# Mixed V written to DRAM and gathered back through the load queue, with the loads and the mixing weights rearranged around it

## The chip, the cores and the metric

The kernel runs on one core of one Trainium2 chip. The metric is the device time of one execution in microseconds (us), smaller being better. A profiled execution gives, beside it, a span (first to last recorded work) and a record of what each engine did. The engines are PE (TensorE matmuls), PEld (its weight loads), DVE (VectorE), ACT (ScalarE), POOL (GpSimd) and SP (SyncE). Loads from DRAM that convert fp32 to fp16 are issued from POOL; plain copies and transposing copies are issued from SP.

## The reference

Two stages follow each other. The first is a block-sorting attention over 4 batches, 8 heads, 768 positions and head size 64; the second a Fourier mixing layer with a layer norm and a two-layer perceptron.

```python
for _ in range(5):                      # P: [4, 8, 8, 8], softmax by rows, then by columns
    P = exp(P - max(P, -1)); P = P / sum(P, -1); P = P / sum(P, -2)
k_sorted = einsum('bhij,bhjcd->bhicd', P, k_blocks)   # blocks of 96 positions
v_sorted = einsum('bhij,bhjcd->bhicd', P, v_blocks)
attn = softmax(0.125 * q_block @ k_sorted_block.T)    # inside each block
x = (attn @ v_sorted_block)                           # -> [4, 768, 512]
mixed = real(fft(fft(x, axis=1), axis=2))
u  = x + mixed
un = (u - mean(u)) / sqrt(var(u) + 1e-6)
out = u + relu(un @ w_ch1) @ w_ch2                    # 512 -> 2048 -> 512
```

## The kernel before, in words

Nothing is written in the order in which it runs. Every step is added to a list (`P.add`) with the engines that may run it, what it reads and writes, a priority and an assumed duration. `Plan.schedule` then lays all steps out in time once, at build time, and the result is one fixed order of instructions per engine. On the chip each engine goes through its own order and waits wherever an input or a buffer isn't ready; later instructions of that engine wait with it. Loads are steps of POOL, plain and transposing copies steps of SP, so POOL's and SP's queues are such fixed orders too. If an assumed duration is wrong, the order stays as it was planned.

The 128 sorted blocks of two batches (2 x 8 heads x 8 blocks) are one group `t` of V. Group 0 serves batches 0 and 1, group 1 batches 2 and 3. The fp16 copy of the raw V has a partition for each source block, and 96 x 64 values in it; group 0 lies in `hr[0]`, group 1 in the first four slots of `kq`, once batch 0's keys and queries have been used.

- `v_path` (L665 on) sums V over its 96 positions: PE adds up pieces of 512 columns with an identity matrix (L675, 12 matmuls a group), DVE reduces the rest (L683) and makes the mean (`vb`, `vbn`). Then V is rearranged into `vcx`: group 0 by eight strided copies (helper line L660) on DVE and ACT, group 1 by eight DVE subtractions of the mean (L708).
- `bdv_make` (L743 on) turns the 8 x 8 sorting weights into block-diagonal matrices with PE (fp32 matmuls, L745) and DVE (L749), and copies them to fp16 (`bdv16`).
- `v_mix` (L713 on) mixes the blocks. For each head-dimension value d a matmul (L724) has the rearranged V as its weights, so that the output has the 96 positions on the partitions, which is what attention needs; group 0 has a second matmul for the mean (L727). Sixteen copies a group (L660, `vsf<-bank`) bring the result to `vsf`, where each block has 64 values and a constant column, a row of 65.
- `kqt` (L897) sorts and transposes the keys, `scores` (L952) multiplies, ACT takes the exponential (L961), DVE or ACT subtract one (L974, L976) and write `eb`, of which there are four. `av` (L991) multiplies with `vsf`, DVE divides (L1003, L1006) and writes `rt`.
- `a_path` and `a_rows` prepare low-rank terms of the transform, `dft1` (L1063 to L1073, with sums on DVE from L1023) and `dft2` (L1138 to L1153) do the two transforms; DVE adds `u` (L1160, L1172), makes statistics (L1186), POOL the inverse deviation (L1193 to L1202, list `lns`), and `un` is normalised (L1213, L1217) and transposed (L1232 by PE for batch 0, a transposing copy on SP for the others).
- `mlp` (L1253 first layer, L1274 second) runs per batch and half of its rows, at a low priority on PE: it fills PE where nothing more urgent is ready.

The loads of keys, queries, V, tables and the perceptron's weights all leave from POOL (L472) in the order keys, queries, V of group 0, further keys and queries, tables, batch 1, weights. Group 1 of V is loaded at about 36 to 40 us, the keys and queries of batches 2 and 3 after the second layer norm of batch 0.

Of the kernel before, what the change touches and what calls it, by code (L numbers as in the profile page):

```python
# [9 lines left out]
F32 = mybir.dt.float32  # L10
# [33 lines left out]
GT = 384  # L44


def _consts():
# [56 lines left out]
    vrow = np.zeros((1, 128, D + 1), f16)  # L104
# [9 lines left out]
    def as32(m):  # L114
# [8 lines left out]
                rows=rows, erow=np.tile(erow, (1, 4)), vrow=vrow, pack=pack)  # L123


class Op:
    __slots__ = ("n", "costs", "fn", "preds", "succs", "left", "ready", "prio",
                 "vts", "fresh", "nbytes", "end", "start", "eng", "tag",
                 "crit", "late")
# [13 lines left out]
class Plan:  # L143
# [14 lines left out]
    def add(self, costs, fn, r=(), w=(), prio=None, nbytes=0, tag="",  # L158
            after=()):
# [7 lines left out]
        o.preds, o.succs, o.vts, o.fresh = set(after), [], [], []  # L167
        for k in r:
            o.preds.update(self.wr.get(k, ()))
# [41 lines left out]
    def schedule(self):  # L211
# [48 lines left out]
        while todo:  # L260
# [70 lines left out]
            for s in o.succs:  # L331
                s.left -= 1
                for x in s.costs:
                    s.ready[x] = max(s.ready[x],
                                     o.end + (0.03 if x == e else self.XL))
# [30 lines left out]
def kernel(  # L366
# [22 lines left out]
    def many(name, n, shape, dtype):  # L389
# [18 lines left out]
    vcx = ct("vcx", [128, 128 * D + 2], F16)  # L408
    dtab = vcx[:, 6144:7168].rearrange("p (c w) -> p c w", c=4)
    lt = vcx[0:97, 7168:7168 + LTW]  # L410
    vsf = ct("vsf", [97, 128 * (D + 1)], F16)
    vsb = vsf[:, 0:128 * (D + 1)].rearrange("p (g w) -> p g w", w=D + 1)
    eb4 = ct("eb4", [97, 4, EW], F16)
    P.pool("eb", [eb4[:, n, :] for n in range(4)])
# [24 lines left out]
             vcx[:, 7938:8194].bitcast(F32).rearrange(  # L439
# [15 lines left out]
    pk = hr[1].rearrange("p a b -> p (a b)")[0:32, 0:1024].rearrange(  # L455
        "p (i x) -> p i x", i=NB)
    pv = hr[1].rearrange("p a b -> p (a b)")[0:32, 1024:3072].bitcast(
        F32).rearrange("p (i x) -> p i x", i=NB)
    pws = hr[1].rearrange("p a b -> p (a b)")[0:32, 3072:3232].bitcast(F32)
# [9 lines left out]
    def load(dst, src, nbytes, w, prio, eng="POOL", r=(), after=()):  # L469
# [3 lines left out]
                  prio=prio, nbytes=nbytes, tag="load", after=after)  # L473
# [3 lines left out]

    slot = {}
# [34 lines left out]
    def load_v(t, hf, prio):  # L513
        load(nat[t].rearrange("p (c d) -> p c d", d=D)[
            :, 48 * hf:48 * hf + 48, :],
            vv[128 * t:128 * t + 128, 48 * hf:48 * hf + 48, :], 1572864,
            [("nat", t, hf)] + (hk(0)[8 * hf:8 * hf + 8] if t == 0 else
                                kqk(2 * hf) + kqk(2 * hf + 1)), prio)
# [10 lines left out]
    for n in range(4):  # L529
        P.add({"POOL": (1.5, 1.6)}, lambda _, n=n: nc.gpsimd.memset(  # L530
            eb4[0:96, n, :], 0.0), w=[("ebz", n)], prio=-190.0, tag="ebz")
# [850 lines left out]
```

The softmax here doesn't subtract the row's maximum and nothing guards it: scores larger than these inputs give would overflow.

## Time and profile before

| what | us |
|---|---|
| median of 14 runs (lowest, highest) | 292.82 (290.82, 294.43) |
| the profiled execution, its own time | 293.97 |
| its span | 292.2 |
| PE busy, of the span | 261.9 |
| DVE busy | 171.3 |
| ACT busy | 157.8 |
| POOL busy | 67.7 |
| first-layer matmuls (L1253), 512 of them | 91.5 |
| second-layer matmuls (L1274), 384 of them | 87.9 |
| mixing of V on PE (L724 and L727), 192 of them | 21.2 |
| mixed V to `vsf` (DVE and ACT, 16 each) | 23.0 |
| subtraction of the mean, group 1 (L708), 8 of them | 11.8 |

A line of a group of instructions gives the line of the code, the engine, the operation, output and inputs, the shape, the count, then the busy time of all and the mean duration in ns of one, and last the idle time of the engine just ahead of them with what ended it. A line of a timeline gives start and duration of one or several equal instructions. Durations of neighbours on one engine overlap a little, so that the distance of two starts is what an instruction costs in a full stretch. A line of the table of stages gives the stage, then the busy time of each engine in it, the granted PE clock (1.00 is full), the mean busy share of the DMA engines and GB/s.

### The profile page before, as it was taken

What the parts mean: (1) busy time and instruction counts of PE and PEld (TensorE: products, weight loads), DVE (VectorE), ACT (ScalarE), POOL (GpSimd) and SP (SyncE); (2) the same over time, 40 slices, a digit from 0 to 9 for tenths busy, and PEclk for the clock granted to TensorE, in tenths of its full rate; (3) what the DMA queues carried; (4) which work ended last, traced back from release to release, by engine and by line L of the source; (5) the groups of instructions that cost most, each with busy time, mean ns of one, the idle gap of its engine ahead of it and who ended that gap; (6) DMA issues with size and microseconds to landing.
All of it is one profiled execution on the core that took longest, in us unless ns stands there. A gap on an engine that the chain in (4) does not pass through costs nothing.

```text
span 292.2 us, 5807 instructions
## 1 busy us (share of the span) xinstructions
PE 261.9 (90%) x2284; PEld 155.6 (53%) x2284; DVE 171.3 (59%) x405; ACT 157.8 (54%) x323; POOL 67.7 (23%) x104
## 2 busy tenths in 40 slices
PE   0289987797999999999999999999999999999980
PEld 0147976554566565554566456455555545545530
DVE  4476899999999999841479742145124226210020
ACT  2485979986778946881368027226514605425300
POOL 8974300003920460020320002023000212200021
PEclk9995999999999999999999999999999999999995
DMA  7999999910991499310112011311321111221001
GB/s 112 211 252 246 213 208 209 221 23 16 96 181 23 73 170 145 78 37 20 72 49 56 2 72 37 57 72 49 46 81 37 38 54 72 38 90 36 2 36 72
DMA packets 42529, 26.33 MB, mean 90 GB/s; under 512 B 30106, under 2 KB 38824, under 8 KB 42500
## 3 DMA queue, kind: packets, MB, share of 16 engines
q0 software_dynamic: 23536, 18.31, 37.2%
q1 hardware_dynamic: 18966, 7.64, 11.7%
q8 instruction: 18, 0.29, 0.4%
q14 instruction: 9, 0.07, 0.1%
HBM read 28.96 MB, written 6.29 MB: 121 GB/s over the span
## 4 chain that ended last, share of the span: by engine, by line
PE 70%; DVE 17%; DMA 7%; issue 3%; POOL 2%; POOLq 0%; ACT 0%; DVEq 0%
PE bank L1274 27%; PE bank L1253 27%; DMA hr<-in_v_dram 5%; DVE rt L1006 2%; PE bank L897 2%; DMA out_dram<-u,rows 2%; PE bank L724 2%; PE bank L991 2%; PE bank L952 2%; PE bank L1149 2%; DVE vsf L660 2%; DVE st L1186 1%; PE bank L1063 1%; DVE eb L974 1%; PE bank L1153 1%
## 5 line engine op out<-in xcount | busy, mean ns | idle before, releaser
L1265 ACT ACTIVATE hr<-bank 128x384 f16<-128x384 f32 x115 | 56.2, 490 | 75.3 <-PE bank L1253 74.5
L1253 PE MATMUL bank<-ut,w1sb 128*128 128x384 f16 x512 | 91.5, 326 | 0.7 <-ACT ut L660 0.7
L1274 PE MATMUL bank<-w2sb,hr 128*128 128x512 f16 x384 | 87.9, 379 | 0.0
L1253 PEld LDWEIGHTS <-w1sb 128*128 128x128 f16 x512 | 48.6, 98 | 34.5 <-issue 1.1
L1274 PEld LDWEIGHTS <-hr 128*128 128x128 f16 x384 | 36.7, 98 | 41.8 <-issue 0.2
L1282 DVE TENSOR_TENSOR u<-bank,u 128x512 f32<-128x512 f32 x24 | 16.5, 689 | 60.2 <-PE bank L1274 59.8
L961 ACT ACTIVATE ex<-bank 96x384 f32<-96x384 f32 x64 | 27.9, 485 | 6.5 <-PE bank L952 6.4
L1295 POOL DMA_INDIRECT out_dram<-u,rows x12 | 12.1, 1011 | 77.0 <-DVE u L1282 56.8
L1193 POOL TENSOR_SCALAR mv<-mv 128x3 f32<-128x3 f32 x8 | 1.9, 239 | 110.6 <-DVE mv L1188 110.6
L976 ACT ACTIVATE eb<-ex,negone 96x384 f16<-96x384 f32 x35 | 20.8, 615 | 0.2
L1213 ACT ACTIVATE un<-u,nm,ny 128x512 f16<-128x512 f32 x15 | 12.2, 810 | 11.5 <-DMA ut<-un 8.2
L472 POOL DMA_DIRECT2D kq<-in_q_dram x20 | 17.4, 896 | 1.7 <-DMA kq<-in_q_dram 1.2
L991 PE MATMUL bank<-vsf,eb 97*128 97x65 f16 x416 | 16.5, 194 | 1.3 <-DVE rr L836 0.5
L1172 DVE SCALAR_TENSOR_TENSOR u<-rt,bank 128x510 f32<-128x510 f16 x12 | 8.1, 680 | 16.3 <-PE bank L1138 8.9
L1006 DVE TENSOR_TENSOR rt<-bank,rz 128x384 f16<-128x384 f32 x32 | 17.3, 550 | 0.3
L991 PEld LDWEIGHTS <-eb 97*128 97x128 f16 x416 | 15.4, 98 | 3.6 <-issue 1.3
L927 PE MATMUL bank<-pack,qr 128*128 128x128 f16 x48 | 5.3, 264 | 13.3 <-ACT qr L660 12.8
L1186 DVE BATCH_NORM_STATS2 st<-u 128x6 f32<-128x512 f32 x24 | 16.1, 686 | 0.3
L1160 DVE SCALAR_TENSOR_TENSOR u<-rt,bank 128x512 f32<-128x512 f16 x12 | 8.0, 684 | 13.9 <-PE bank L1153 13.5
L724 PE MATMUL bank<-bdv,vcx 128*128 128x128 f16 (+1 forms) x128 | 12.7, 226 | 0.0
L952 PE MATMUL bank<-qt,ks 64*128 64x96 f16 x256 | 11.5, 209 | 1.3 <-DVE rt L1006 0.4
L660 DVE CAST vsf<-bank 96x512 f16<-96x512 f32 x16 | 11.5, 776 | 1.3 <-PE bank L727 1.2
(130 smaller groups left out, 342.3 us busy)
## 6 DMA issues: line engine op xcount, KB each, us to landing
kq<-in_k_dram POOLq DMA_DIRECT2D x8, 384.0 KB, 7.2
w1sb<-in_moe_w_ch_dram POOLq DMA_DIRECT2D x4, 512.0 KB, 15.4
w2sb<-in_moe_w_ch_dram POOLq DMA_DIRECT2D x4, 512.0 KB, 18.8
out_dram<-u SPq DMA_DIRECT2D x8, 256.0 KB, 2.0
kq<-in_q_dram POOLq DMA_DIRECT2D x4, 384.0 KB, 11.3
hr<-in_v_dram POOLq DMA_DIRECT2D x2, 768.0 KB, 12.3
kq<-in_v_dram POOLq DMA_DIRECT2D x2, 768.0 KB, 20.7
kq<-in_q_dram POOLq DMA_DIRECT2D x16, 96.0 KB, 5.3
```

Of the source, the lines that this page charges most:

```text
L472: o = P.add({eng: c}, lambda _: e.dma_start(dst, src), r=r, w=w, prio=prio, nbytes=nbytes, tag="load", after=after)
L660: (nc.scalar.copy if e == "ACT" else V.tensor_copy)(dst, src)
L724: nc.tensor.matmul(o, vcx[:, 96 * d:96 * d + m], bd, start=True, stop=(t == 1))
L952: nc.tensor.matmul(pss[h2].ap[:, BLK * j:BLK * j + BLK], ks.ap[rows, 4 * g + j, :], qt.ap[rows, c0:c0 + BLK])
L961: nc.scalar.activation(ex.ap, pss[h2].ap[0:96, 0:384], AF.Exp, scale=SCALE),
L976: nc.scalar.activation(ed, src, AF.Identity, bias=negone[0:96])
L991: nc.tensor.matmul(po.ap[:, 65 * T:65 * T + 65], eb.ap[:, e0:e0 + 128], vsf[:, vi:vi + 65], start=(n == 0), stop=(n == len(WIN[T]) - 1), s ...
L1006: P.add({"DVE": (0.45, 0.56)}, lambda _: V.tensor_tensor(rt.ap[:, :, D * h:D * h + D], po3()[:, :, 0:D], rz.ap[:, :, None].broadcast_to([1 ...
L1186: P.add({"DVE": (0.6, 0.69)}, lambda _, u=u, st=st: V.bn_stats(st.ap, u.ap), r=[u], w=[st], tag="bn")
L1253: nc.tensor.matmul(ps.ap[:, 0:GT], w1sb[:, c, 128 * fc:128 * fc + 128], ut.ap[:, c, :], start=(c == 0), stop=(c == 3))
L1265: nc.scalar.activation(hr[g][:, fc, :], ps.ap[:, 0:GT], AF.Relu)
L1274: nc.tensor.matmul(ps.ap, hr[g][:, fc, 128 * tt:128 * tt + 128], w2sb[:, fc, :], start=(fc == 0), stop=(fc == 15))
```

## The change

1. Mixing on PE uses the weights the other way round: the block-diagonal matrix is the stationary operand and V streams, 512 columns at a time. A group has 12 pieces (group 0 two matmuls for each, the second for the mean), and the output has the blocks on the partitions. The rearranging copies into `vcx` are gone, and `vcx` is small.
2. The result is therefore transposed as far as attention is concerned. It is copied to SBUF (`vm`: `hr[1]` for group 0, in place for group 1), written to DRAM by six copies on SP for each group, and gathered back into `vsf` by six transfers on POOL, each of 32 x 64 rows of 64 fp16 values. `av` of a batch waits for the three transfers of its half. Rows of `vsf` are 80 wide.
3. Loads: V of group 0 goes first, then the queries and keys of batch 0 and half of batch 1. Tables, the other half of batch 1 and the weights stand in POOL's queue behind the first three gathers (`gate`, `behind`).
4. V of group 1 is loaded after the second layer norm of batch 0, by six transfers of 128 x 16 rows of 64 values; its sum over positions moves from PE to four DVE reductions, and the subtraction becomes two instructions in place.
5. The mixing weights become fp16 parts: high and low halves come from the fp32 weights, PE multiplies both in fp16, and `bdv16` and `bdv32` both come straight from PSUM.
6. `eb` has six buffers instead of four; the clearing of two is on DVE. The sorting weights' scratch space moves from `hr[1]` to `rv`, `fo`, `eo` and `rr`. Priorities of `dft2` and of batch 1's low-rank terms change, and two of `dft2`'s matmul groups are held behind the third.

```diff
-    load_qk("k", 0, 0, -5000.0)
-    load_qk("q", 0, 0, -4999.0)
-    load_v(0, 0, -4998.0)
-    load_v(0, 1, -4997.0)
+    load_v(0, 0, -5000.0)
+    load_v(0, 1, -4999.0)
+    load_qk("q", 0, 0, -4998.0)
+    load_qk("k", 0, 0, -4997.0)
     load_qk("k", 0, 1, -4996.0)
     load_qk("q", 0, 1, -4995.0)
...
+    load_qk("k", 1, 0, -4994.0)
+    load_qk("q", 1, 0, -4993.0)
...
+        if t:
+            for n in range(4):
+                P.add({"DVE": (1.65, 1.75)}, lambda _, n=n: V.tensor_reduce(
+                    vb[:, 0, 16 * n:16 * n + 16],
+                    n3.rearrange("p c d -> p d c")[:, 16 * n:16 * n + 16],
+                    axis=AX.X, op=ALU.add),
+                    r=[("nat", 1, r) for r in range(6)] + stage, w=["vb"],
+                    tag="vb1")
...
+        for hf in range(2):
+            def f(_, hf=hf):
+                m = nat[1][:, 3072 * hf:3072 * hf + 3072].rearrange(
+                    "p (c d) -> p c d", d=D)
+                V.tensor_tensor(m, m, vbn[:, None, :].broadcast_to(
+                    [128, 48, D]), op=ALU.subtract)
...
-        for n in range(16):
+        for n in range(12):
+            r, hf = divmod(n, 2)
             ps = Buf("pm", "pf")
...
+                nc.tensor.matmul(o, bd, n4[:, r, 8 * hf:8 * hf + 8],
+                                 start=True, stop=(t == 1))
+                if t == 0:
+                    nc.tensor.matmul(
+                        o, bd, vbn[:, None, :].broadcast_to([128, 8, D]),
+                        start=False, stop=True)
...
+        for hb in range(2):
+            w64 = slice(64 * hb, 64 * hb + 64)
+            for k_ in range(3):
+                cols = slice(2048 * k_, 2048 * k_ + 2048)
+                P.add({"SP": (0.4, 4.2)}, lambda _, w64=w64, cols=cols:
+                      nc.sync.dma_start(vdr[t][w64, cols], vm[w64, cols]),
...
+                o = P.add({"POOL": (1.3, 1.3)},
+                          lambda _, k_=k_, w64=w64, cols=cols:
+                          nc.gpsimd.dma_start(
+                              vsb[32 * k_:32 * k_ + 32, w64, 0:D],
+                              vdr[t][w64, cols].rearrange(
+                                  "g (c d) -> c g d", d=D)),
...
-              + [("vsb", n) for n in range(16)], w=[po, (rts[b], "a", h)],
+              + [("vsb", n, b % 2) for n in range(3)],
...
+    gate = gets[0, 0][-1:]
+    for n, nm in enumerate(("dtab", "lt", "tab", "cs")):
+        load_c(nm, 25.0 + n)
+    load_qk("k", 1, 1, 31.0)
+    load_qk("q", 1, 1, 31.5)
...
+    gate = lns[1:2]
     load_v(1, 0, 60.0)
     load_v(1, 1, 61.0)
+    gate = ()
```

## The prediction

> **What bounds the kernel now.** I read the table of stages first, to see where PE is full and where it isn't.
>
> ```profile
> core 0: us, PE busy (x) PEld busy (x) DVE busy (x) ACT busy (x) POOL busy (x), PEclk, DMA share, GB/s
> 45.00:50.00 5.00, 3.79 (x73) 2.96 (x74) 5.00 (x16) 5.00 (x12) 0.00 (x0) 1.00 1.24 207
> 60.00:65.00 5.00, 4.44 (x59) 3.03 (x58) 5.00 (x11) 4.18 (x11) 0.00 (x0) 1.00 0.01 3
> 120.00:140.00 20.00, 20.00 (x147) 10.41 (x146) 8.30 (x19) 11.35 (x26) 2.71 (x5) 1.00 0.16 32
> ```
>
> There are two regimes. Up to some 75 us DVE is full (5.00 of 5.00) and PE has holes; afterwards PE is full and DVE isn't. The PE timeline has the border, the chain of waits the end (start, us, what):
>
> ```profile
> 73.20 1.46 PE L1253 MATMUL bank<-ut,w1sb 128*128 128x384 f16 x8 [0.67 <-ACT ut L660]
> ```
>
> ```profile
> 274.98 4.33 PE bank L1274 x20
> ```
>
> The last matmul ends at about 279.4; 12.8 us of output follow, to 292.2. From 73.2 to 279.4 are 206.2 us. PE's instructions behind the border, counted in the built order and priced by distances of starts in full stretches (L1253 3.90/24 = 0.163 us, L1274 7.77/36 = 0.216, the small ones likewise), need 202.2 us. So the span is the time of the first L1253, plus 202.2, plus some 4 of holes, plus 12.8. What must be forecast is the border, the work behind it, and the holes. For the border I read DVE's timeline and the start of the chain, which comes first here:
>
> ```profile
> 3.54 13.84 DMA hr<-in_v_dram
> ```
>
> ```profile
> 39.21 0.18 DVE L1003 RECIPROCAL rz<-bank 128x6 f32<-128x6 f32 x1
> 62.72 1.87 DVE L1160 SCALAR_TENSOR_TENSOR u<-rt,bank 128x512 f32<-128x512 f16 x3
> 69.16 0.55 DVE L1217 TENSOR_SCALAR un<-u,ny,nm 128x512 f16<-128x512 f32 x1
> ```
>
> V lands at 17.4, attention's first division comes at 39.2, the first u at 62.7, the first un at 69.2, the first layer 4.0 later.
>
> **What the Trainium skill says.** "DMA: Bandwidth & Descriptors" (Anatomy of one DMA) says that DMA engines don't wait on semaphores: the issuing engine waits, and what is queued on it waits too. The trace has it: POOL sits 15.9 us ahead of a key load, waiting for L724. The same section gives a fixed 2.0 us for a POOL-issued DMA; here they take longer, 4.5 to 5.4 us from the start of the issue for query loads of 96 KB, and the trace decides. Its "Two DMAs through the same engine are not ordered" says that a DMA reading what another wrote must wait for its semaphore: store and gather can't overlap. "TensorE: Matmul & The Clock Gate" (Part 1) says that PE runs at half rate until it has been busy for some 3.4 us; before 29 us a 512-column matmul takes 0.416 (2.50/6), later 0.216.
>
> **The change part by part.**
>
> *Loads first.* Two V loads now have nothing ahead of them. Before, the first query load had landed at 10.05, half of V at 13.7, all at 17.4: 1.57 MB each 3.67 us. So V lands at 13.7, 3.7 earlier; query and key of batch 0 at 15.5 and 17.4, all eight loads at about 25. The sorting weights no longer wait behind query copies on ACT (a hole of 2.99 on DVE) and are done at about 11.6, before V. Hidden by V.
>
> *Mean and weights.* Six matmuls after V's landing (2.5), the reduction 0.7, small work: `vbn` at 18.3. The fp16 weight matmuls replace fp32 ones of 0.29 each and lie beside query transposes; likewise two more DVE memsets lie where DVE waits for the first load. Nil; uncovered, 1 to 2 us.
>
> *Mix.* From about 18.7, 24 matmuls at 0.416 until the clock rises, then 0.216: 5.2 to 10 us. I take a rise at about 23 and the last copy at 26.6 (12 copies of 0.58 on ACT or 0.68 on DVE, rows of 64x512 casts). Removed: 128 matmuls, eight rearrangements (8.5 us on two engines) and 16 copies of 0.78; added those 12.
>
> *Store and gather.* No such row exists. Store: 256 KB output copies on SP land after 2.0; bounds 1.8 and 3; last of the first half at 28.8. Gather: 2048 rows of 128 B. Query loads have 768 such rows and leave POOL each 0.83 us, landing no later within a burst (POOL's timeline, then the DMA issues: count, size, us to landing):
>
> ```profile
> 79.01 3.32 POOL L472 DMA_DIRECT2D kq<-in_q_dram  x4
> ```
>
> ```profile
> kq<-in_q_dram POOLq DMA_DIRECT2D x4, 96.0 KB, 5.3
> ```
>
> So DMA passes at least 925 rows a us: at most 2.2 us for a gather; from the slope of the issue (512 rows 0.745, 768 rows 0.83) at least 1.4. A further 4.4 until landing. The third lands at 28.8 + 1.4..2.2 + 4.4 = 34.6 to 35.4. Meanwhile scores go on, which six `eb` permit. DVE's work from the first mix copy to the first division is 15.5 (5 copies of V, 4 of keys, 3 of queries, 7 subtractions, low-rank steps and others): from 19.6, not before 35.1. With holes while PE is cold I take 36.5 for the division, against 39.2: the gather is just hidden.
>
> *From there to u.* Before 23.5, all DVE. Gone from this stretch, by starts: four divisions 1.8 and reciprocals 0.4, two `bdk` 2.2, two query copies 1.8, two key copies 1.0, three subtractions 0.8, low-rank steps 1.0: 9.0, leaving 14.7. They don't vanish: part moved ahead, under the gather's latency, part behind the border, where DVE isn't full. With 0.5 for chain latency, u at 51.7. From u to un 6.4 and from un to the first L1253 4.0 as before: **62.1, not 73.2; 11.1 earlier.**
>
> *Loads behind the gathers.* Everything queued on POOL behind the third gather (tables, half of batch 1, second gathers, weights) starts at 30.6, not at 13.6. 3.1 MB at 0.43 MB/us, 4 to land: tables by 38, while the transform starts at about 46. Gathers, then 4.2 MB: first-layer weights by 56 to 58, second-layer by 66, wanted at 62 and 77. Hidden, with 4 us to spare at the tightest.
>
> *PE behind the border.* 64 mix matmuls of 0.056 (3.6) become 12 of 0.216 (2.6); 26 attention and 8 score matmuls, 1.0 together, slip behind the border. Again 202.2: nil.
>
> *Group 1.* Its loads now wait for the layer norm, border + 1. Six of 2048 rows: 8.4 to 13.2 on POOL, landing at +14 to +18.6; batch 2's keys and queries queue behind. Then four reductions of 1.5 to 1.9 (1536 values, from a copy of 768 at 0.75 and a reduction of 512 at 0.65), two residual sums queued between, 1.3: done at +22 to +27.5. The subtraction is 1.9 (four times a 768-value sum of 0.47) or 3.4 (a broadcast of 1024 at 1.12, times three); I take 1.9. PE's order has mixing after 27.3 us of work, so at +27 to +30 with holes; the second three pieces later. Nil to 3. The last gather starts behind the layer norm of batch 1 at about +41 and lands at +46 to +48; attention of batch 2 comes after 46.4 of work plus holes. Nil to 2. Waits on SP behind the stores (query transposes) meet later users. I take 2 more holes, 6 in all; bounds 1 and 9.
>
> *Sum.* 62.1 + 202.2 + 6 + 12.8 = 283.1 against a span of 292.2: 9.1 less, 284.9 for the profiled execution of 293.97. That lies 1.15 above the median, so 292.82 - 9.1 = **283.7**.
>
> **The rivals.**
>
> *Short rows are slow* (slower than before). Gathers and V loads of group 1 move 128-byte rows. For: 20 times 2048 is far more than any load before, and no transfer had more than 768; 32 partitions are a new form. Against: the 925 rows a us, with DVE full. With X us for 2048 rows the third gather lands at 24.5 + 3X + 4.4, and group 1's V at +5.4 + 6X. X = 4 gives 40.9 (4.4 late) and +29.4, reductions and subtraction until +39, some 11 of holes: 283.1 + 15.4 = 298.5, about 299. It decides from X of about 3.2.
>
> *Half the gain lost in dependencies*: PE stays cold through the mix and the fixed order couples PE, ACT and DVE: division at 40, holes 8: 283.1 + 3.5 + 2 = 288.6, about 289. For: ACT and PE each have 10 us of work between mix and division. Against: before, DVE lost only 1.5 of 49 us there.
>
> *Given back later*: the border moves, but group 1's chain (load, reduction, mix, store, gather) costs 9 of holes beyond the usual 4 and 2: no change, 292.8. For: the chain has five hand-overs through POOL and SP in a fixed order. Against: 20 us of other PE work lie ahead of it.
>
> **How the numbers follow.** About 0.3% (0.9 us) can be told from no change. Forecast 0.60, lost in dependencies 0.18, given back 0.06, slow rows 0.16. Faster is the first two, 0.78; within 0.3% most of the third, 0.05; slower the fourth and a little of the third, 0.17. The likeliest case alone spans 279 to 288. Some 0.06 lies under 279, from warm PE and few holes; 0.12 lies above 295 in the slow-row case. So 279 to 295.
>
> **What would show it.** V landing near 13.7; gathers of at most 2.2 us each; the first division at about 36 and the first L1253 at about 62; PE full behind it with about 6 us of holes, most around group 1's mix and batch 2's attention. Wrong: gathers landing more than 8 us after issue, DVE idle in front of L707, or first-layer matmuls waiting for weights.

## The result, and the profile after

The changed kernel takes 297.56 us (median of 10 runs, 293.83 to 299.22), against 292.81 (47 runs) before: a ratio of 1.0127, 95% interval 1.0095 to 1.0159. It is slower by 1.3%; I had forecast 283.7. Executions over 1.5% above the fastest of the same kernel count as a slower state: the medians of this document hold all timed runs, the ratios leave those out, and there is no ratio where too few remain.

The profiled execution took 300.37 us (span 298.6), 2.8 over the median, so sizes are checked below against a second profiled execution of the same kernel (297.76, span 296.0). The stages that were shown of before, now of the changed kernel:

```profile
core 0: us, PE busy (x) PEld busy (x) DVE busy (x) ACT busy (x) POOL busy (x), PEclk, DMA share, GB/s
45.00:50.00 5.00, 3.15 (x71) 2.39 (x70) 4.44 (x14) 4.26 (x12) 1.65 (x3) 1.00 1.07 156
60.00:65.00 5.00, 3.99 (x62) 2.59 (x58) 4.86 (x12) 4.33 (x10) 1.59 (x4) 0.83 1.23 206
120.00:140.00 20.00, 17.46 (x200) 9.44 (x200) 9.16 (x24) 9.68 (x21) 8.27 (x10) 0.91 1.55 161
```

The border is the change of regime at the first first-layer matmul, 73.20 before. In front of it DVE is now a little short of full (4.44 and 4.86 of 5.00). From 120 to 140, where PE had 20.00 of 20.00, it now has 17.46 at a granted clock of 0.91, and the DMA share (next to last column) has gone from 0.16 to 1.55; it adds up packets that are under way at once, so it can pass 1. The two large DMA queues tell of the same (last column: time of their packets as a share of 16 engines' span); 37.2% and 11.7% before:

```profile
q0 software_dynamic: 36592, 21.46, 49.9%
q1 hardware_dynamic: 19926, 10.80, 15.8%
```

The border and the last piece of PE work in the PE timeline and the chain that ended last (start, us, what):

```profile
69.05 1.47 PE L1326 MATMUL bank<-ut,w1sb 128*128 128x384 f16 x8
```

```profile
279.93 6.06 PE bank L1347 x28
```

73.2 became 69.05: 4.1 won of 11.1 forecast. From 69.05 to the tail of 12.8 are 216.7 us, for 202.2 of work: holes of 14.6, where before there were 4 (second execution: border 69.36, holes 296.0 - 12.8 - 69.36 - 202.2 = 11.6). So the span of 298.6 lies 15.5 over the forecast of 283.1, 6.95 by the border and 8.6 by the holes; in the second execution it is 12.9, by 7.3 and 5.6.

Holes are a remainder, and two things are in it: time in which PE does nothing, and work that takes PE longer than its price. From the border to PE's last matmul PE was idle for 1.6 us before, for 7.7 in the changed kernel and 6.5 in its second execution. It was busy for 208.9 us before, and for 213.5 and 211.8 after, with some 15 matmuls fewer; the granted clock from the border on was 1.00 before, 0.98 and 0.99 after.

DVE's timeline, in the lines that answer to those of before:

```profile
38.32 0.17 DVE L1073 RECIPROCAL rz<-bank 128x6 f32<-128x6 f32 x1
57.91 1.44 DVE L1233 SCALAR_TENSOR_TENSOR u<-rt,bank 128x512 f32<-128x512 f16 x2 [2.85 <-PE bank L1225]
64.61 0.55 DVE L1290 TENSOR_SCALAR un<-u,ny,nm 128x512 f16<-128x512 f32 x1
```

The first division came at 38.32 (39.21 before, 36.5 forecast), u at 57.91 (62.72; 51.7). In front of u DVE stood idle for 2.85 us, waiting for L1225 of PE. PE's timeline says for what, and gives the two large holes behind the border (in brackets: idle time, and what ended it):

```profile
57.50 0.38 PE L1225 MATMUL bank<-rb,vcx 97*128 97x512 f16 x1 [2.53 <-DMA rb<-rv]
...
122.20 0.20 PE L1021 MATMUL bank<-qt,ks 64*128 64x96 f16 x1 [3.16 <-ACT ex L1030]
...
143.61 1.44 PE L1326 MATMUL bank<-ut,w1sb 128*128 128x384 f16 x4 [2.28 <-DVE u L1355]
```

Each is one step away from a DMA. The first waits for the four small copies of low-rank rows, `rb`. Behind the second stands ACT, behind the third DVE; their timelines:

```profile
120.96 0.81 ACT L1286 ACTIVATE un<-u,nm,ny 128x512 f16<-128x512 f32 x1 [4.30 <-DMA ut<-un]
```

```profile
141.34 0.69 DVE L1245 SCALAR_TENSOR_TENSOR u<-rt,bank 128x510 f32<-128x510 f16 x1 [3.96 <-DMA out_dram<-u,rows]
```

ACT may not write the third normalised tile `un` before a transposing copy has read the first (there are two buffers); DVE may not write `u` before an output has left: the first indirect output (rows scattered to DRAM from POOL) landed 7.6 us after its issue, 2.9 before. SP's queue shows the company in which those transposing copies start:

```profile
103.64 8.49 SPq L782 DMA_DIRECT2D vdr<-kq  x6
...
112.30 2.00 SPq L984 DMA_TRANSPOSE qt<-kq  x1
114.40 8.68 SPq L1297 DMA_TRANSPOSE ut<-un  x3
```

Six stores of the second group, then a query transpose, then the copies; from 112.9 to 119 POOL issues its last four gathers, then batch 3's loads. The first of the three copies left at 114.40 and ACT went on at 120.96, 6.6 us later. Before, the same copies (L1224) ran at 128 to 134 with hardly another DMA about (a DMA share of 0.28, their own), and the one whose landing the trace has took 2.5 us.

### The profile page after: what moved, and what is told of

Its sections match the earlier page's. It is cut to its first block, busy times and chain, and to the rows that moved or that the text cites. A ratio compares the mean times of both kernels' runs of the same rounds, so it can differ in the third digit from the quotient of the medians.

```text
span 298.6 us, 5526 instructions
## 1 busy us (share of the span) xinstructions
PE 262.5 (88%) x2124; PEld 147.9 (50%) x2124; DVE 175.2 (59%) x407; ACT 145.2 (49%) x307; POOL 85.2 (29%) x120
## 4 chain that ended last, share of the span: by engine, by line
PE 48%; DMA 4%; DVE 1%; issue 1%; POOLq 0%; DVEq 0%
PE bank L1326 21%; PE bank L1347 20%; DMA out_dram<-u,rows 4%; PE bank L1221 1%; PE bank L1133 1%; PE bank L1060 1%; PE bank L1021 1%; PE bank L1225 1%; DVE u L1355 0%; POOLq L1467 0%; PE bank L966 0%; PE bank L1209 0%; PE bank L1138 0%; DVE u L1245 0%; PE bank L1143 0%
## 5 line engine op out<-in xcount | busy, mean ns | idle before, releaser
L1326 PE MATMUL bank<-ut,w1sb 128*128 128x384 f16 x512 | 93.6, 329 | 2.8 <-DVE u L1355 2.6
L1347 PE MATMUL bank<-w2sb,hr 128*128 128x512 f16 x384 | 90.1, 386 | 0.0
L1338 ACT ACTIVATE hr<-bank 128x384 f16<-128x384 f32 x109 | 53.2, 490 | 72.5 <-PE bank L1326 71.6
L1326 PEld LDWEIGHTS <-w1sb 128*128 128x128 f16 x512 | 48.7, 98 | 37.7 <-issue 4.7
L1347 PEld LDWEIGHTS <-hr 128*128 128x128 f16 x384 | 37.5, 99 | 43.5 <-issue 3.1
L1030 ACT ACTIVATE ex<-bank 96x384 f32<-96x384 f32 x64 | 28.3, 485 | 10.6 <-PE bank L1021 10.1
L788 POOL DMA_DIRECT2D vsf<-vdr x12 | 13.2, 1101 | 35.3 <-DMA vdr<-kq 22.1
L1060 PE MATMUL bank<-vsf,eb 97*128 97x65 f16 x416 | 17.8, 201 | 2.2 <-DMA vsf<-vdr 1.0
L1045 ACT ACTIVATE eb<-ex,negone 96x384 f16<-96x384 f32 x31 | 18.5, 614 | 0.3
L486 POOL DMA_DIRECT2D kq<-in_q_dram x20 | 16.4, 835 | 6.7 <-DMA kq<-in_k_dram 2.4
L1286 ACT ACTIVATE un<-u,nm,ny 128x512 f16<-128x512 f32 x15 | 12.2, 811 | 11.3 <-DMA ut<-un 10.0
L1021 PE MATMUL bank<-qt,ks 64*128 64x96 f16 x256 | 12.5, 214 | 3.9 <-ACT ex L1030 3.3
L718 PE MATMUL bank<-hr,pack 128*128 128x512 f16 x12 | 5.4, 623 | 10.5 <-DMA hr<-in_v_dram 10.5
L966 PE MATMUL bank<-bdk,kq 128*64 128x128 f16 x192 | 11.3, 233 | 2.8 <-ACT ex L1030 1.6
```

The costliest lines, as they stand in the source:

```text
L486: o = P.add({eng: c}, lambda _: e.dma_start(dst, src), r=r, w=w, prio=prio, nbytes=nbytes, tag="load", after=after, behind=gate)
L788: nc.gpsimd.dma_start(vsb[32 * k_:32 * k_ + 32, w64, 0:D], vdr[t][w64, cols].rearrange("g (c d) -> c g d", d=D)),
L1021: nc.tensor.matmul(pss[h2].ap[:, BLK * j:BLK * j + BLK], ks.ap[rows, 4 * g + j, :], qt.ap[rows, c0:c0 + BLK])
L1030: nc.scalar.activation(ex.ap, pss[h2].ap[0:96, 0:384], AF.Exp, scale=SCALE),
L1045: nc.scalar.activation(ed, src, AF.Identity, bias=negone[0:96])
L1060: nc.tensor.matmul(po.ap[:, 65 * T:65 * T + 65], eb.ap[:, e0:e0 + 128], vsf[:, vi:vi + 65], start=(n == 0), stop=(n == len(WIN[T]) - 1), s ...
```

## The experiments

Border means the start of the first L1326 matmul (L1253 in the kernel before) in the run's own profile; holes mean span less border, less 202.2 of PE work, less 12.8 of tail; "PE idle" is the part of them in which PE does nothing, from the border to its last matmul. Every run had runs of the kernel before beside it (medians 292.92 to 293.93), and the ratio is to these. The theories: **A**, the second group's stores and gathers make the holes behind the border, through transfers that lie beside them; **B**, that group's slow reductions do; **C**, late low-rank rows delay the border; **D**, short rows are what makes gathers dear; **E**, the planner's durations are wrong; **F**, the second group's V is loaded too late. In the diffs, `put(order, a, b)` takes operations a out of the planned order and sets them behind b.

| run | median us (runs) | ratio to before (95%) | border | holes | PE idle |
|---|---|---|---|---|---|
| before | 292.81 (47) |  | 73.2 | 4.0 | 1.6 |
| changed | 297.56 (10) | 1.0127 (1.0095, 1.0159) | 69.05 | 14.6 | 7.7 |
| after_again | 298.22 (6) | 1.0160 (1.0118, 1.0202) | 69.36 | 11.6 | 6.5 |
| no_store_gather | 292.15 (20) | 0.9959 (0.9936, 0.9983) | 67.89 | 7.3 | 2.5 |
| stores_only | 298.18 (4) | 1.0167 (1.0095, 1.0239) | 67.83 | 12.5 | 6.3 |
| third_un | 300.05 (4) | none | 69.98 | 11.3 | 5.4 |
| half_reduce | 298.99 (4) | 1.0232 (1.0181, 1.0282) | 69.66 | 10.0 | 5.6 |
| gathers_late | 297.27 (15) | 1.0094 (1.0057, 1.0131) | 68.05 | 10.5 | 6.8 |
| gathers_late_un | 298.16 (4) | 1.0182 (1.0128, 1.0235) | 67.65 | 11.5 | 6.6 |
| pe_transpose | 297.73 (4) | 1.0153 (1.0088, 1.0218) | 67.65 | 12.6 | 4.9 |
| pe_transpose_u | 296.50 (4) | 1.0135 (1.0094, 1.0175) | 67.75 | 11.3 | 4.0 |
| gather_alone | 310.70 (1) | none | 66.74 | 27.2 | 16.9 |
| rows_other_data | 297.11 (4) | 1.0145 (1.0098, 1.0192) | 66.17 | 11.9 | 6.3 |
| neither | 290.41 (6) | 0.9895 (0.9853, 0.9936) | 67.28 | 6.1 | 2.3 |
| w2_late | 302.22 (4) | 1.0303 (1.0209, 1.0397) | 68.08 | 15.5 | 8.6 |
| weights_behind_rows | 300.81 (4) | 1.0255 (1.0215, 1.0296) | 68.03 | 16.7 | 9.4 |
| all_mended | 303.87 (6) | 1.0280 (1.0242, 1.0318) | 67.27 | 22.0 | 14.0 |
| plan_measured | 307.77 (4) | 1.0504 (1.0468, 1.0539) | 72.91 | 17.9 | 11.1 |
| v_of_2_early | 304.35 (5) | 1.0375 (1.0327, 1.0424) | 72.99 | 11.6 | 6.7 |
| before_v_first | 298.13 (4) | 1.0155 (1.0108, 1.0202) | 76.94 | 4.9 | 2.3 |

**The spread.** First the changed kernel once more.

> The changed kernel once more, nothing edited, beside the others on the same chip, for the spread of its stages: first division at 36 to 38.5, border at 66.5 to 70, holes behind the border 10 to 15 (span less border, 202.2 and 12.8); the time 297 to 299.

As expected, but for the first division, 38.90. Nine profiled executions whose code in front of the border is the same (changed, after_again, no_store_gather, stores_only, third_un, half_reduce, gathers_late, gathers_late_un, gather_alone) have it at 66.7 to 70.0, mean 68.5; their first division lies at 37.9 on the mean, u at 56.9. Holes of one kernel differ by 3 (14.6 and 11.6), PE idle by 1.2. Differences within that are not read as effects below, single profiles of the border least of all.

### The traffic of the second group

`no_store_gather`, in the loop that emits the planned operations:

```
+ if o.tag in ("vst", "vgt") and o.n > 400: continue
```

> Leaves out the six stores and six gathers of the second group (batches 2 and 3 then read the mixed V of batches 0 and 1), everything else in its place. Theory A (the second group's stores stand on SP ahead of the transposes of batch 1, its gathers on POOL ahead of batch 3's loads, and the two holes of PE at 119-122 and 141-144 with the half clock behind each come from that): both holes go, 7 to 10 us less than the changed kernel, 288 to 291. Theory B (the reductions and the mixing itself make the second group late): the holes stay, at most 2 us less. The border (first L1326 matmul) stays at about 69 in either case.

5.4 us less, 0.9959 of before, and holes of 7.3: theory A, though I had given it 7 to 10. PE is idle for 2.5 us instead of 6.5 to 7.7, and of the two large holes one is left, the first, at 1.01 in the PE timeline:

```profile
119.24 0.20 PE L1021 MATMUL bank<-qt,ks 64*128 64x96 f16 x1 [1.01 <-ACT ex L1030]
```

`stores_only` leaves out the gathers alone (`o.tag == "vgt"`).

> Leaves out the six gathers of the second group and keeps its six stores (batches 2 and 3 then read the mixed V of batches 0 and 1). Theory A1 (the gathers, by what they do to the transfers beside them, make the holes): as without stores and gathers, holes behind the border 6 to 8.5, 291 to 293. Theory A2 (the stores' place on SP ahead of the transposing copies makes them): holes stay at 10 or more, 296 or later.

298.18, 12.5 of holes and 6.3 of PE idle, so A1 falls: the gathers aren't all of it. Nor is it that attention waits for the gathered data, which here it doesn't. The second hole is gone, but the first is larger than ever:

```profile
122.07 0.85 PE L1021 MATMUL bank<-qt,ks 64*128 64x96 f16 x8 [5.00 <-ACT ex L1030]
```

With no gathers ahead of them, batch 3's loads leave POOL at 109.9 to 119.7, over the transposing copies, and ACT waits 6.14 us for the first of them. In `no_store_gather` these loads leave at nearly the same time, 111.0 to 119.3, and ACT waits 2.15. So the stores do harm without the gathers, beside loads that alone do little. A2 named their place on SP; that it is this place is not shown.

`third_un` gives the third tile `un` a buffer of its own, `gathers_late` puts batch 3's three gathers behind its loads and the first indirect output, and `gathers_late_un` does both:

```
+ if o.n == 533:
+     o.fresh[0].ap = spare
+ order = put(order, [473, 475, 477], 1001)
```

> The third normalised row tile of batch 1's first group has a buffer of its own, so that ACT no longer waits for the transposing copy of the first one; the order is untouched. Theory A in its narrow form (the wait of ACT for that buffer, 4.3 us, is what stops PE at 119-122): that hole and the half clock behind it go, 4 to 6.5 us less than the changed kernel. Rival: scores and attention of batch 2 are late anyway (the next gather or transposing copy ends last) and the hole only moves: less than 2 us.

> The three gathers of the second group that serve batch 3 alone move on POOL behind the loads of batch 3 and the first indirect output; stores and all else as they were. Theory A in the form of contention (these short-row gathers keep the DMA engines busy while transposing copies, loads and outputs want them): key and query loads of batch 3 start some 3 us earlier, the first indirect output lands in about 3 us instead of 7.6 and the hole at 141-144 goes, 3 to 5 us less than the changed kernel. Rival (the hole at 119-122 is the order of SP and the rest follows from it): less than 1.5 us.

> Both edits together: the separate buffer for the third normalised tile and the three gathers of batch 3 behind its loads. Theory A: both holes go, and with them 6 to 9 us of the changed kernel, as with the second group's traffic left out altogether: 289 to 292, level with or a little faster than before. Rival: the remaining stores and gathers of batch 2 keep a hole in front of its attention, at least 3 us of it stay.

The first hole goes with the spare tile, but PE then stops 0.93 for a gather and 3.20 at 141; with the late gathers alone it stops at 120 (1.96) and 144 (1.79), and with both edits at 136 (1.48) and 143 (2.86). Holes are 10.5 to 11.5 in all three. `gathers_late` may have won about 1 us (1.0094, against 1.0127 and 1.0160, intervals that overlap), the others nothing. My 6 to 9 us for both failed: where one hole goes, another comes.

`pe_transpose` puts batch 1's transposes on TensorE, for which the planner lays the whole order anew; `pe_transpose_u` also gives a tile of its own to the first `u` of batch 1's second group:

```
- if b > 0:
+ if b > 1:
      P.add({"SP": (1.3, 4.0)}, lambda _, tt=tt, un=un:
...
+ if o.n == 539:
+     o.fresh[-1].ap = spare_u
```

> Batch 1's six transposes of normalised tiles go through TensorE, as those of batch 0 do, instead of through DMA; the planner lays the order anew. It adds 24 matmuls of 128 columns and six copies, about 1.5 us of PE. Theory A (transposing copies slowed by the second group's traffic stop PE): the hole at 119-122 goes, 1 to 4 us less than the changed kernel. Rival (something else is late there as well): no gain, or 1 to 2 us more.

> Batch 1's transposes on TensorE, and a tile of its own for the first u of batch 1's second group, which otherwise waits for the indirect output of the tile before. If these two waits are all: no hole over 1.5 us behind the border, holes 6 to 8.5 in all (1.5 of it added PE work), 290.5 to 293.5 as a median. If the traffic makes new waits: holes at 10 or more, 296 or later.

The first hole goes in `pe_transpose`, the other is 3.72 there (its holes contain some 1.5 of added PE work, so compare PE idle: 4.9 and 4.0). In `pe_transpose_u` the wait for an output moves to the next `u`; DVE's timeline:

```profile
141.40 0.69 DVE L1247 SCALAR_TENSOR_TENSOR u<-rt,bank 128x510 f32<-128x510 f16 x1 [3.20 <-DMA out_dram<-u,rows]
```

So these two waits aren't all. PE idle comes down, but the ratios, 1.0153 and 1.0135, are those of the changed kernel.

`gather_alone` measures the transfer itself, in two late stages without the second group's traffic: six gathers, then six copies of the same data in rows of 4 KB.

```
+ if o.n == 745:
...
+     nc.gpsimd.dma_start(vsb[32 * k_:32 * k_ + 32, w64, 0:D],
+         vdr[1][w64, cols].rearrange("g (c d) -> c g d", d=D))
+ if o.n == 881:
...
+     nc.gpsimd.dma_start(vsf[32 * k_:32 * k_ + 32, 4096 * hb:
+             4096 * hb + 4096].rearrange("p (b x) -> p b x", b=2),
+         vdr[1][w64, cols].rearrange("(p b) x -> p b x", b=2))
```

> Adds six gathers of 256 KB in rows of 128 bytes on POOL behind the first layer norm of batch 2, and six copies of the same data in rows of 4 KB behind that of batch 3, into the mixed V's place when nobody reads it any more (no other DMA of weight is near). Theory D (short rows cost the DMA engines far more time than their bytes): a gather takes about 2 us of all 16 engines, the last of six lands some 13 us after the first issue; wide copies about 0.7 to 1 us each. Rival (a gather costs what its issue shows, 1.05 us): both kinds land at the pace of their issue, 6 to 8 us for six. The end is unchanged within 1 us.

The end came 12.9 us later than in after_again's profile, not unchanged, and neither stage was quiet: each batch's transposing copies and outputs fell into it. DMA issues (count, size, median us to landing) from 207 to 230 with the gathers, then from 239.5 to 262 with the wide copies:

```profile
vsf<-vdr POOLq DMA_DIRECT2D x6, 256.0 KB, 8.8
out_dram<-u SPq DMA_DIRECT2D x2, 256.0 KB, 7.3
ut<-un SPq DMA_TRANSPOSE x3, 7.8
```

```profile
vsf<-vdr POOLq DMA_DIRECT2D x6, 256.0 KB, 8.5
ut<-un SPq DMA_TRANSPOSE x3, 12.9
out_dram<-u,rows POOLq DMA_INDIRECT x3, 7.7
```

The gathers' packets took 50.3% of the 16 engines' time over 23 us, 1.9 us of all of them each; the wide copies, with three outputs on the same queue, 51.4% over 22.5. Wide rows land as late and cost as much, so theory D has nothing for it here: in this company the row's length makes no difference. What a gather costs with no other DMA about, no run shows.

What both have in common is what they do to their neighbours. Of the three transposing copies in each stretch the trace has one landing: 7.8 us beside the gathers, 12.9 beside the wide copies, 2.5 when alone. PE stops for each of them, 6.10 and 4.86 us. The plain outputs fare no better, 7.3 where alone they take 2.0. The Trainium skill ("Advanced Engine Details and Errata", X-Bar Transpose (TRN2)) says that transposing DMAs are as fast as regular ones. Alone they come near it here (128 KB in 2.5 us, a plain output of 256 KB in 2.0), and beside the gathers both are slow alike (7.8 and 7.3), so it doesn't look as if the transposing were what slows them. In the changed kernel the 6.6 us between the first copy and ACT's return are 4.1 more than 2.5, nearly all of the 4.30 that ACT waits in front of the first hole.

### Reductions, V loads and the planner

`half_reduce` reads 48 of the 96 columns at L707:

```
- n3.rearrange("p c d -> p d c")[:, 16 * n:16 * n + 16],
+ n3.rearrange("p c d -> p d c")[:, 16 * n:16 * n + 16, 0:48],
```

> The four reductions of the second group's V read half of their columns (so the mean is not the right one): about 1.4 us each instead of 2.75, 5.4 us less of DVE. Theory B (their size makes the second group late): its chain starts 5 us earlier and the end comes 3 to 6 us earlier. Theory A: vbn comes 5 us earlier, but the order on SP stays, and at most 2 us are won.

A reduction took 1.41 instead of 2.73, and 298.99 is no gain. But the chain didn't start 5 us earlier either, as I had expected under both theories: on DVE two sums of outputs stand between the third reduction and the fourth, and DVE waited for them:

```profile
93.02 0.69 DVE L1356 TENSOR_TENSOR u<-bank,u 128x512 f32<-128x512 f32 x1 [4.41 <-PE bank L1348]
```

The fourth began at 94.49 (93.73 in the changed kernel), and the first store left SP at 103.32 (103.64). So the size of the reductions isn't what sets the group's dates, and in that sense B falls. What an earlier group would be worth, this run doesn't tell. `v_of_2_early` moves the six loads:

```
+ order = put(order, [427, 428, 429, 430, 431, 432], 135)
```

> The six V loads of the second group are issued right behind the second-layer weights, at about 55, and not behind the first layer norms at 70. Theory F (loading V of batches 2 and 3 behind the layer norms makes the group late): reductions no longer wait 1.7 us, the reads of batch 2 start earlier, 1.5 to 4 us less than the changed kernel. Theory A: the order of DVE sets when the reductions run, within 1 us of the changed kernel.

6.1 slower than after_again, through something I hadn't seen. POOL's timeline:

```profile
61.43 1.14 POOL L499 DMA_DIRECT2D kq<-in_v_dram  x1 [1.37 <-DMA w2sb<-in_moe_w_ch_dram]
64.38 1.14 POOL L499 DMA_DIRECT2D kq<-in_v_dram  x1 [1.81 <-DMA w2sb<-in_moe_w_ch_dram]
65.60 0.25 POOL L1279 TENSOR_SCALAR mv<-mv 128x3 f32<-128x3 f32 x1
```

Five of the six V loads leave POOL 0.53 to 0.56 us after the landing of the load that stands eight places ahead in its queue (of the sixth that landing isn't in the trace). In this run, the changed kernel and the kernel before, no load or gather leaves POOL while eight are under way. The layer norm, queued behind the six, starts at 65.6, though the first u had started at 54.36; `un` comes 13.1 us after u instead of 6.5. So loading early costs more than it wins. F itself isn't tested: the reductions began 14.6 us behind the border, 15.4 in the changed kernel, so the group was hardly earlier.

`plan_measured` gives the planner measured durations (L707's reduction, L782's store, L788's gather, the transposing copy, the rows; each old value above, the new one below):

```
- {"DVE": (1.65, 1.75)}  {"SP": (0.4, 4.2)}  nbytes=690000   {"SP": (1.3, 4.0)}  {"SP": (0.1, 2.3)}
+ {"DVE": (2.7, 2.8)}    {"SP": (0.9, 5.2)}  nbytes=1000000  {"SP": (1.3, 7.0)}  {"SP": (0.6, 2.3 if b else 7.0)}
```

> No instruction is taken away or added; only the durations that the planner assumes are changed to measured ones (reduction of the second group's V 1.65 to 2.7, store 4.2 to 5.2, gather's bytes so that it takes 2.5 us, transposing copy 4.0 to 7.0, small row copies of batch 0 2.3 to 7.0), so the whole order is laid anew. Theory E (the fixed order is wrong because it was laid with too short durations): the waits of PE and DVE on DMAs shrink, 3 to 7 us less than the changed kernel. Rival (the traffic itself is what costs, any order meets it): within 2 us of the changed kernel or slower.

The slowest of all but `gather_alone`, 307.77. A fixed duration can't say that a transfer takes long only in company, which may be why; it isn't shown. So E isn't shown by this, and that no order is better isn't either.

### The border

`rows_other_data` skips the four copies L928 of batch 0, and fills `rb[0:96]` from the table `cs` at the start:

```
+ if o.n in (247, 248, 249, 250): continue
...
+ nc.sync.dma_start(rb[0:96, :], cn["cs"].ap().rearrange(
+     "p a b c -> p (a b c)")[0:96, 0:DM])
```

> Leaves out the four small copies of batch 0's low-rank rows; those rows are filled at the start of the kernel from a table in HBM instead, so that the first matmul that reads them has nothing to wait for. Theory C (the small copies, slowed to over 7 us by the loads behind the gathers, delay the first layer norm): the wait of 2.5 us on PE and the idle 2.9 us of DVE at 55-58 go, u starts at 54 to 55.5 and the border (first-layer matmul) comes 2.5 to 4 us earlier, at 65 to 67; the end 1 to 3 us earlier. Rival (DVE's own order and a cold PE set the border): the border moves by less than 1.2 us.

Border at 66.17, and DVE's idle time ahead of u is down to 0.16:

```profile
54.14 1.34 DVE L1233 SCALAR_TENSOR_TENSOR u<-rt,bank 128x512 f32<-128x512 f16 x2 [0.16 <-PE bank L1225]
```

From the first division to u are 17.24 us, 17.26 in `neither`, against 19.0 on the mean of the nine: the rows cost about 1.75. The nine spread from 16.9 to 19.8, so the mean carries this, with one thing more: in each of the nine PE waits for a DMA of rows ahead of its first L1225 (0.41 to 2.53 us), and u starts 0.4 after that matmul. C holds for the border, which comes 2.3 before the mean (1.2 in `neither`), less than the 2.5 that I gave it at least. At the end nothing of it is left to see: 1.0145, against 1.0127 and 1.0160, where I had expected 1 to 3 us. `w2_late` (its line is the first) and `weights_behind_rows` try to speed the copies, the one by moving the second-layer weights behind the first layer norm, the other by moving all weights behind the rows:

```
+ order = put(order, [132, 133, 134, 135], 291)
...
+ order = put(order, [128, 129, 130, 131, 132, 133, 134, 135], 250)
+ if o.n == 250: nc.gpsimd.tensor_copy(held[0:96], rb[0:96, 0:1])
```

> The four loads of second-layer weights move on POOL from behind the first-layer weights to behind the first layer norm. Theory C (they fill the DMA engines while the four small copies of low-rank rows are under way, which PE waits for at 57.5): those copies land in 2 to 3 us instead of 7.3, the wait of 2.5 goes, the border comes 2 to 4 us earlier, and the end 0 to 4 us earlier, depending on what is given back at the second group. Rival: the copies are slow for another reason, or the weights become late: border unchanged, or a new wait in front of the second layer.

> The eight loads of first- and second-layer weights move on POOL behind a small copy that reads the low-rank rows of batch 0, so that they start when those rows have landed (about 51 instead of 40). Theory C: the small copies land in 2 to 3 us, u comes at 53.5 to 55, and since the weights still land by 62 to 64 the border comes 2 to 3 us earlier than in the changed kernel, at 65 to 66.5. Rival: the first-layer weights become what ends last, border at 67 or later, with the first-layer matmul waiting for a DMA.

Both borders come near 68, half a us below the mean, which is within the spread. In `w2_late` the copies still had the first-layer weights beside them (one landed after 8.1 us, and PE waited 1.66). In `weights_behind_rows` one landed after 1.8 us, all by 52.9, and first division to u is 17.6: it is the weights beside them that make the copies slow. But the border doesn't profit, though no first-layer matmul waits for a DMA. The loads of the second group, queued behind, come later, and PE stops at 97 (1.65 in `w2_late`, 2.93 in the other). Both end slower. `all_mended` joins the edits of `weights_behind_rows`, `third_un` and `gathers_late` with the spare `u` (for operation 536).

> Four edits together: weights behind the low-rank rows, a buffer of its own for the third normalised tile of batch 1 and for the first u of its second group, batch 3's gathers behind the first indirect output. Theory A and C together: border at 65 to 67, holes behind it 6 to 9 instead of 10 to 15, 287.5 to 291.5 as a median, so faster than both. Rival (holes move to the next transfer that is late, as in the run with two of these edits): holes stay at 10 or more, 293 or later.

It is 303.87 (1.0280). In the profiled execution, 306.07, to the late V of the second group comes a hole of 8.83 at 153, in front of a score matmul. The rival was right: the holes moved.

`neither` has the edits of `rows_other_data` and `no_store_gather`.

> Leaves out the copies of batch 0's low-rank rows (filled early with other data) and the second group's stores and gathers (batches 2 and 3 read batches 0 and 1's mixed V). If the two causes add: border 65.5 to 67, holes 6 to 8.5, so a span of 287 to 290 and 288.5 to 291 as a median, 6 to 9 below the changed kernel. If they share a cause: no better than the run with the traffic alone left out, 292.

290.41, ratio to before 0.9895, holes 6.1; the border, 67.28, is a little later than hoped. The ratio lies 0.6% under that of `no_store_gather`, with intervals that meet at 0.9936. That fits two causes which add, but since the rows alone won nothing at the end, it doesn't show it.

`before_v_first` is the kernel before with both V loads ahead:

```
- load_qk("k", 0, 0, -5000.0)
- load_qk("q", 0, 0, -4999.0)
- load_v(0, 0, -4998.0)
- load_v(0, 1, -4997.0)
+ load_v(0, 0, -5000.0)
+ load_v(0, 1, -4999.0)
+ load_qk("k", 0, 0, -4998.0)
+ load_qk("q", 0, 0, -4997.0)
```

> The kernel before with one part of the change alone: both V loads of the first group ahead of batch 0's keys and queries; mixing and all else as before (the planner lays the order anew). If the earlier V carries the gain: V lands at about 13.7 instead of 17.4, the border comes 2 to 4 us earlier than 73.2 and the end likewise, 289 to 291. If the 9 us of copies and mixing work of DVE that the change removes carry it: keys and queries come later, the border moves by less than 1 us, 292 to 294.

Neither of my two cases: 298.13, slower by 1.6%, with the first division at 43.07 and the border at 76.94. In the kernel before, V ahead of the keys by itself costs. Whether it pays in the changed kernel, no run here shows.

## Why the prediction was wrong, step by step

Two steps failed: the start of u, 51.7, which came at 56.9 on the mean of nine, and the holes behind the border, 6, which became 14.6 and 11.6.

*Loads first; mean and weights.* Right: the second half of V lands at 13.2 (13.7 forecast), `vbn` comes at 17.9 (18.3), the last mixing copy ends at 25.7 (26.6).

*Store and gather.* The gather was right, the store too small. Stores of the first group land 3.7 to 4.2 us after their issue, not the 2.0 that I took from outputs, above my bound of 3. The three gathers that the first division waits for leave POOL each in 1.05 to 1.41 and land after 6.1 to 6.5, in the 5.8 to 6.6 that I had. Their bound of 925 rows a us rested on a loose reading, though: the burst of query loads at 79 lands 5.3, 5.4, 5.0 and 6.3 us after issue, so the last does land later. The third gather could only start at 30.6 and landed at 37.0, 1.6 after my latest date. So it isn't hidden: PE waits 1.0 us for it, and the first division comes at 38.3, on the mean of nine at 37.9, not 36.5.

*From there to u.* It failed here first. DVE's work between division and u was sized nearly right (15.3 busy in `rows_other_data` against 14.7 forecast, which should have been 14.5 by its own terms, 23.5 less 9.0). But I moved only what stands on DVE ("all DVE"), and took the other input of u, the low-rank rows, along without looking. They didn't move: the copies leave SP at 47.1 to 49.1 before and at 47.6 to 50.0 after. In the landings that the traces have they took 5.7 and 6.5 us before, 7.3 after and 5.5 in the second execution: hidden when u is due at 62.7, not when it is due at 52. The profile of before had it: with rows that leave at 49 and land 6 later, u can't start at 51.7. With the mean of nine, the border is 6.4 late: 1.4 by the division, 1.75 by the rows, 2.05 by other waits and work up to u, 1.2 from u on. The last two are remainders without a run that takes them apart. PE's granted clock may be in both: from 40 to 60 it was 1.00 before, 0.84 and 0.85 in the two executions after, and from 60 to 75, where the transposes are, 0.77 in six of the nine.

*Loads behind the gathers: "Hidden".* Hidden, but with nothing to spare. First-layer weights landed by 62.6, not 58, and second-layer weights by 73.0, not 66; no first-layer matmul waited for them, since the border was at 69 and not at the forecast 62.1. And I didn't cost what else is in the DMA engines while they run: the rows.

*PE behind the border, 202.2.* The matmuls are what they were but for some 15, yet PE took longer over them: 213.5 and 211.8 us busy, for 208.9 before. One reading under the sum was wrong: 279.4 is the end of the last matmul of the chain that ended last; PE's own last matmul ends at 283.6. The holes are defined by the same sums in every run, so comparing them isn't touched.

*Group 1: "nil to 3", "nil to 2", two more holes, bounds 1 and 9.* This is the larger failure: holes of 14.6 and 11.6, against 6 forecast and 4 before, past the bound of 9; without the group's stores and gathers they were 7.3. Of the chain's own members the subtraction was right (1.76 against 1.9), the reduction too small (2.73 against 1.5 to 1.9). The last gather landed 57 us behind the border, not 46 to 48. Yet PE never waited for these gathers behind the border in the changed kernel; its two large holes are behind a transposing copy, which lies beside this traffic, and an output, which lies beside batch 3's loads: these leave POOL at 119.0 to 132.1, behind the gathers, and at 111.0 to 119.3 where stores and gathers are left out. I followed one chain to its own dates and asked who waits for it; I should have asked whose transfers it lies beside. "Waits on SP behind the stores (query transposes) meet later users" was one line, and the layer norm's transposing copies, on the same queue, weren't in it.

*The rivals.* The number of "short rows are slow", 299, came near by luck: its mechanism found no support, since a gather takes 1.9 us of the engines, under the 3.2 from which it was to decide, and wide rows did no better. "Lost in dependencies" and "given back later" were each half right, and they aren't alternatives: the border lost 7, the holes another 6 to 9, and I had given them chances as if only one could be. Of my three signs of error one showed: three later gathers of the first group landed 12.7 to 14.7 us after their issue and one of the second after 8.4, over the bound of 8. DVE idled 1.67 ahead of L707, and no first-layer matmul waited for weights.

**What stays open.** What makes copies slow beside other transfers isn't settled; the share of stores, gathers and loads in it neither, since leaving out one brings forward the next. Whether holes would shrink if the second group came earlier isn't tested. Of the 10.6 us of added holes 6.2 are idle PE, and some 4.6 are PE work at a slower pace; how much of that pace follows from the holes isn't shown. Nor is it shown that no order of this work beats the kernel before: of the kernels here only `no_store_gather` and `neither` do, and both leave work out.

## What to carry to other kernels

When a change routes data through memory, count the time that it takes of all DMA engines, not only when its own data are due, and list every small copy, transpose and output that will be under way with it: each may be what another engine waits for. When you move a border forward, check each input of the first operation behind it against its own time of arrival in the trace; one that was hidden by the old border doesn't move along. If one wait taken away brings up the next, stop mending waits and take away traffic.

## What the runs showed of the hardware

- Transposing copies of 128 KB: 2.5 us alone; beside six POOL transfers of 256 KB 7.8 (short rows) and 12.9 (long ones), one landing each. Plain outputs of 256 KB: 2.0 alone, 7.3 beside the same short rows.
- In the traces of the kernel before, the changed one and `v_of_2_early` no load or gather leaves POOL while eight are under way: the next goes 0.28 us or more after the landing of the load eight places ahead, 0.53 to 0.56 for the V loads of the second group. POOL stood still for 0.95 to 1.81 us ahead of each of these in `v_of_2_early`, and all that was queued behind stood too. Whether the chip sets the eight or the way in which the program waits isn't shown.
- Small copies of 16 to 32 KB on SP: 1.8 us without weights beside them (`weights_behind_rows`), 5.5 to 8.1 beside loads of weights.
- After a hole PE is slow as well, but not always. Behind the hole of 3.16 in the changed kernel eight L1347 matmuls took 3.26 us, behind one of 2.25 in the second execution 1.89. PE timelines of the two:

```profile
123.81 3.26 PE L1347 MATMUL bank<-w2sb,hr 128*128 128x512 f16 x8
```

```profile
123.50 1.89 PE L1347 MATMUL bank<-w2sb,hr 128*128 128x512 f16 x8
```

- A reduction along a strided direction, 1536 fp16 values into 16, takes DVE 2.73 us, 0.56 values a ns and partition.
